# Thresholded attention and a three-way maxout feed-forward on one core: every engine's instructions put into an order written by hand

## The chip, the core and the metric

The kernel runs on one core of a Trainium2 chip. The metric is the device time of one execution in microseconds (us); lower is better. The engines are TensorE (PE in the profile, with its weight loads as PEld), VectorE (DVE), ScalarE (ACT), GpSimd (POOL) and SyncE (SP), which here only issues transfers.

## What is computed

Attention over 8 batches of 8 heads, 576 positions, head size 64, where scores more than `tau` = 0.02 below their row's maximum are dropped, and then a feed-forward layer whose hidden value is the maximum of three products:

```python
scores = scale * np.matmul(q, k.transpose(0, 1, 3, 2))
thresh = np.max(scores, axis=-1, keepdims=True) - tau
scores = np.where(scores >= thresh, scores, -1000000000.0)
scores = scores - np.max(scores, axis=-1, keepdims=True)
attn = np.exp(scores)
attn = attn / (np.sum(attn, axis=-1, keepdims=True) + 1e-09)
out = np.matmul(attn, v)                      # (8, 8, 576, 64)
x = out.transpose(0, 2, 1, 3).reshape(4608, 512)
h = np.maximum(np.maximum(x @ w1, x @ w2), x @ w3)   # 4608 x 768
y = h @ w_out                                 # 4608 x 512
```

## The kernel before

**Tiling.** The work goes by *quads*: four heads of one batch, so two quads to a batch and 16 in all. A quad is two pairs of heads (`pr` 0 and 1), and its scores are made in nine *chunks* (`idx` 0 to 8): 128 query rows of both heads of a pair, and in chunk 4 the last 64 rows of each head of both pairs. A chunk has two halves, `i` = 1 and then `i` = 0, one for each head. A half is a 128 x 576 tile of scores.

**A half's steps.** `scores` makes it in two matmuls that run side by side in the upper and the lower 64 rows of the array: one writes 256 columns and the other 320 (for `i` = 1 the upper rows write 256, for `i` = 0 they write 320). Each is recorded as two passes. Then `exponents`: VectorE takes the row maximum `nm`, and ScalarE reads the scores from PSUM into `z`. This has two forms. In the *plain* form VectorE adds `tau` to the maximum (`bm`), ScalarE applies a Prelu with a huge slope, and `numerators` is a second ScalarE pass, an exponential with a row sum. In the *masked* form ScalarE takes the exponential at once, and `numerators` is a VectorE SCALAR_TENSOR_TENSOR that drops what is under the threshold and sums. `MASKED` lists the chunks that take the masked form. Then `normalized`, once a chunk: a reciprocal on VectorE, two multiplications on GpSimd into `P` (bf16), and one DMA transpose of `P` into `ptq`, issued by SyncE.

**Other steps.** `transposed` (PSUM tile `tp`) turns q or k of a head pair by matmuls with the identity; four of them make the next quad ready. `product` (tile `o`) multiplies a head pair's `ptq` with v; two for each quad, of the quad before. `hid` (tile `ph`, 18 a batch) is one of the three hidden products for 128 of 768 columns, eight matmuls: the first of three (`wi` 0) is copied to `hm` by ScalarE, the others are folded in with a maximum by VectorE. `outp` (tile `po`, 5 a batch) makes 128 rows of the output, which ScalarE copies to `ob`.

**Order.** The loop goes over quads `g` and 18 periods `per` of a quad, one half each. In a period `other(g, per)` adds one other step: `product` for quad `g-1` at periods 3 (`O_A`) and 8 (`O_B`), `transposed` for quad `g+1` at 10, 12, 14, 16 (`T_AT`), and else the next `hid` or `outp` waiting in `todo`. A batch's 23 feed-forward steps come into `todo` after the second product of its second quad. GpSimd alone keeps the written order (`_Ordered`); on the other engines the framework's scheduler places the instructions.

**Buffers.** All PSUM tiles come from one pool of four slots that goes round (`slot`), so a tile waits until the tile four before it has been read. `z` has four buffers, `P` four, `ptq` two.

Of the kernel before, what the change touches and what calls it, by code (L numbers as in the profile page):

```python
# [11 lines left out]
F32 = mybir.dt.float32  # L12
BF16 = mybir.dt.bfloat16
AX = mybir.AxisListType.X
AF = bass_rust.ActivationFunctionType
# [4 lines left out]

STEEP = -1.0e30

MASKED = (1, 4, 7)
LAG = 0


class _Ordered:
# [20 lines left out]
def kernel(  # L48
# [18 lines left out]


    nc = tc.nc
    tensor, scalar, vector, pool = nc.tensor, nc.scalar, nc.vector, _Ordered(tc, nc.gpsimd)  # L70
    B, H, S, D = q.shape
    scale = 1.0 / math.sqrt(D)
    tau = float(tau)
# [4 lines left out]
    W = 2 * S  # L78
# [24 lines left out]
    def slot(name):  # L103
        return ps_s.tile([128, 1024], F32, name=name, tag="s")
# [52 lines left out]
    def scores(L, idx, i):  # L157

        ps = slot("sc")
        first = 256 if i == 1 else 192  # L160
        for r in range(2):
            cols = slice(first, 512) if r == 0 else slice(512, first + S)
            if i == 1:
                kc = slice(0, 256) if r == 0 else slice(0, 320)
            else:
                kc = slice(256, 576) if r == 0 else slice(320, 576)
            rows = slice(64 * r, 64 * r + 64)
            if idx != 4:
# [3 lines left out]
                tensor.matmul(ps[:, cols], t[rows, off:off + 128], L["kt", pr][rows, kc],  # L172
                              start=True, stop=True)
            else:
                for pr in range(2):
                    t = L["qt", pr] if i == r else L["qs", pr]
                    tensor.matmul(ps[64 * pr:64 * pr + 64, cols], t[rows, 256:320],  # L177
                                  L["kt", pr][rows, kc], start=True, stop=True)
        return ps[:, first:first + S]

    def exponents(L, idx, i, sc):

        masked = idx in MASKED
        n = 1 - i
        if n == 0:
            L["z"] = zz.tile([128, W], F32, name="z")
            L["sm"] = small.tile([128, 2], F32, name="sm")
        zn = L["z"][:, n * S:(n + 1) * S]
        nm = small.tile([128, 1], F32, name="nm")
        vector.tensor_reduce(out=nm, in_=sc, axis=AX, op=OP.max, negate=True)  # L190
        if masked:
            scalar.activation(out=zn, in_=sc, func=AF.Exp, bias=nm)  # L192
        else:
            bm = small.tile([128, 1], F32, name="bm")
            vector.tensor_scalar_add(bm, nm, tau)  # L195
            scalar.activation(out=zn, in_=sc, func=AF.Prelu, bias=bm, alpha=-STEEP)  # L196

    def numerators(L, idx, i, z, sm):
        masked = idx in MASKED
        n = 1 - i  # L200
        zn = z[:, n * S:(n + 1) * S]
        acc = sm[:, n:n + 1]
        if masked:
            vector.scalar_tensor_tensor(out=zn, in0=zn, scalar=thr, in1=zn,  # L204
                                        op0=OP.is_ge, op1=OP.mult, accum_out=acc)
        else:
            scalar.activation(out=zn, in_=zn, func=AF.Exp, accum_out=acc)  # L207

    def normalized(L, idx, z, sm):
        rs = small.tile([128, 2], F32, name="rs")  # L210
        vector.reciprocal(rs, sm)  # L211
# [104 lines left out]
    sc = scores(Ls[0], 0, 1)  # L316
    late = []
    for g in range(NQ):
        L = Ls[g]
        L["pt"] = pt_pool.tile([128, 9, W], BF16, name="ptq")  # L320
        for per in range(18):
            idx, i = per // 2, 1 - per % 2
            if per == 0 and g + 1 < NQ:
                Ls[g + 1] = load(*quads[g + 1])
            if per == 2 and g == 0:
                cast_v(Ls[0])
            if per == 6 and g + 1 < NQ:
                cast_v(Ls[g + 1])
            exponents(L, idx, i, sc)
            if per < 17:  # L330
                sc = scores(L, (per + 1) // 2, 1 - (per + 1) % 2)
            elif g + 1 < NQ:
                sc = scores(Ls[g + 1], 0, 1)
            late.append(lambda L=L, idx=idx, i=i, z=L["z"], sm=L["sm"]: numerators(L, idx, i, z, sm))
            if i == 0:
                late.append(lambda L=L, idx=idx, z=L["z"], sm=L["sm"]: normalized(L, idx, z, sm))
            if LAG:
                while len(late) > LAG:
                    late.pop(0)()
            other(g, per)  # L340
            if not LAG:
                while late:
                    late.pop(0)()
            if wl and (g or per >= 6) and per % 2:
                wl.pop(0)()
    while late:
        late.pop(0)()
    while todo:
        todo.pop(0)()
    o_step(NQ - 1, 0)  # L350
    o_step(NQ - 1, 1)
    while todo:
        todo.pop(0)()

# [34 lines left out]
```

## Time and profile before

| | |
|---|---|
| median of 3 runs | 574.15 us (571.12 to 575.34) |
| profiled execution | 570.12 us |
| its span, first to last instruction | 568.3 us |
| mean granted TensorE clock | 0.987 |
| busy: PE / DVE / ACT / POOL | 541.7 / 429.6 / 415.8 / 316.0 us |
| instructions | 10605 |
| 128 x 576 row maximum on VectorE | 288, 749 ns each |
| DMA transposes | 144, 3.4 us to landing |

Rows of the timeline give start, duration, engine, source line, operation, the tile written and the tile read, and in brackets how long the engine sat idle before and what ended that. Records of matmuls overlap, because the next starts before the one ahead of it has left the array; what a step costs TensorE is therefore the time from its start to the start of the next step, not the sum of its records.

### The profile page before, as it was taken

The numbers are of one execution on the slowest core, as the hardware profiler recorded it, in microseconds if no ns is written. First come the engines' busy times: TensorE is split into PE (matmuls) and PEld (weight loads), VectorE is DVE, ScalarE is ACT, GpSimd is POOL, SyncE is SP. The second block draws the span as 40 slices with busy tenths as digits, with TensorE's granted clock in tenths as the row PEclk, the third lists the DMA queues.
The fourth block names the chain that finished last, engine by engine and source line by source line (L and its number), as shares of the span: only waits on it lengthen the run. The fifth ranks groups of instructions, "written<-read, shape, count | busy, mean of one in ns | idle before, by whom it ended". The sixth has DMA issues, their size and how long they took to land.

```text
span 568.3 us, 10605 instructions
## 1 busy us (share of the span) xinstructions
PE 541.7 (95%) x3619; PEld 280.1 (49%) x3632; DVE 429.6 (76%) x976; ACT 415.8 (73%) x809; POOL 316.0 (56%) x408
## 2 busy tenths in 40 slices
PE   7786789999999999999999999999999999999997
PEld 4343445554555545554455544555455554555473
DVE  2985878886787868878788876888688786887441
ACT  2995978687877877778787778868787787777422
POOL 2798886564565646466565555646456565643300
PEclk9996989999999999999999999999999999999999
DMA  7999997758686675957868487774889446444602
GB/s 214 218 219 245 237 213 158 136 92 217 136 175 115 134 191 125 174 110 168 201 124 135 111 206 165 139 148 96 197 154 164 79 82 157 85 84 76 155 1 83
DMA packets 217109, 84.05 MB, mean 148 GB/s; under 512 B 185568, under 2 KB 212448, under 8 KB 217056
## 3 DMA queue, kind: packets, MB, share of 16 engines
q1 hardware_dynamic: 214464, 80.24, 66.9%
q0 software_dynamic: 2592, 3.15, 3.6%
q8 instruction: 28, 0.46, 0.4%
q14 instruction: 25, 0.20, 0.1%
HBM read 34.60 MB, written 9.44 MB: 77 GB/s over the span
## 4 chain that ended last, share of the span: by engine, by line
PE 79%; DVE 8%; ACT 6%; issue 3%; DMA 2%; SPq 1%; POOL 0%; POOLq 0%; ACTq 0%
PE sc L172 28%; PE ph L259 26%; PE tp L143 9%; PE o L236 8%; PE po L272 7%; DVE nm L190 4%; ACT z L207 2%; DVE z L204 2%; ACT z L196 2%; PE sc L177 2%; DMA ptq<-P 2%; ACT ob L275 1%; DMA km<-in_k_dram 1%; ACT xt L243 1%; ACT z L192 0%
## 5 line engine op out<-in xcount | busy, mean ns | idle before, releaser
L36 POOL TENSOR_SCALAR P<-z,rs 128x576 bf16<-128x576 f32 x288 | 236.1, 832 | 191.0 <-DVE rs L211 95.2
L190 DVE TENSOR_REDUCE nm<-sc 128x1 f32<-128x576 f32 x288 | 215.3, 749 | 42.4 <-PE sc L172 33.0
L172 PE MATMUL sc<-kt,qt 64*128 64x256 f32 (+1 forms) x512 | 191.6, 459 | 3.5 <-ACT z L196 3.4
L172 PE MATMUL sc<-kt,qs 64*128 64x320 f32 (+1 forms) x512 | 191.9, 459 | 3.1 <-ACT z L192 2.2
L196 ACT ACTIVATE z<-sc,bm 128x576 f32<-128x576 f32 x192 | 140.8, 736 | 68.4 <-DVE bm L195 39.7
L259 PE MATMUL ph<-xt,w 128*128 128x288 bf16 x1152 | 164.2, 287 | 0.3
L259 PEld LDWEIGHTS <-w 128*128 128x128 bf16 x1152 | 102.2, 98 | 79.0 <-issue 56.8
L207 ACT ACTIVATE z<-z 128x576 f32<-128x576 f32 x192 | 131.0, 683 | 4.2
L204 DVE SCALAR_TENSOR_TENSOR z<-z 128x576 f32<-128x576 f32 x96 | 84.1, 877 | 17.4 <-ACT z L192 16.3
L172 PEld LDWEIGHTS sc<-kt,qs 64*128 64x128 f32 x512 | 77.6, 188 | 35.9 <-ACT z L207 10.9
L192 ACT ACTIVATE z<-sc,nm 128x576 f32<-128x576 f32 x96 | 70.6, 735 | 30.8 <-DVE nm L190 29.9
L172 PEld LDWEIGHTS sc<-kt,qt 64*128 64x128 f32 x512 | 77.6, 188 | 31.2 <-issue 12.2
L36 POOL COPY qs<-qt 64x576 f32<-64x576 f32 x64 | 49.3, 770 | 28.0 <-ACT qt L147 25.3
L272 PE MATMUL po<-wo,hT 128*128 128x512 bf16 (+1 forms) x227 | 57.3, 381 | 0.7
L236 PE MATMUL o<-ptq,vb 128*64 128x288 bf16 (+2 forms) x512 | 46.2, 301 | 5.0 <-DMA ptq<-P 3.3
L266 DVE TENSOR_TENSOR hm<-ph,hm 128x576 bf16<-128x576 f32 x48 | 36.2, 755 | 15.5 <-PE ph L259 12.9
L263 ACT ACTIVATE hm<-ph 128x576 bf16<-128x576 f32 x48 | 31.0, 646 | 19.1 <-PE ph L259 19.1
L211 DVE RECIPROCAL rs<-sm 128x2 f32<-128x2 f32 x144 | 23.4, 162 | 22.1 <-ACT z L207 20.6
L266 DVE TENSOR_TENSOR hT<-ph,hm 128x576 bf16<-128x576 f32 x48 | 36.3, 757 | 3.3 <-PE ph L259 1.1
L272 PEld LDWEIGHTS <-hT 128*128 128x128 bf16 (+1 forms) x240 | 21.2, 100 | 34.9 <-issue 14.7
L236 PEld LDWEIGHTS <-vb 128*64 128x64 bf16 x512 | 25.4, 112 | 25.4 <-issue 17.2
L207 ACT ACTIVATION_READ_ACCUMULATOR z<-z 128x1 f32 x192 | 36.5, 190 | 0.0
(33 smaller groups left out, 360.6 us busy)
## 6 DMA issues: line engine op xcount, KB each, us to landing
vm<-in_v_dram SPq DMA_DIRECT2D x16, 512.0 KB, 4.7
out_dram<-ob SPq DMA_DIRECT2D x32, 256.0 KB, 2.7
qm<-in_q_dram SPq DMA_DIRECT2D x15, 512.0 KB, 4.5
km<-in_k_dram SPq DMA_DIRECT2D x15, 512.0 KB, 4.8
ptq<-P SPq DMA_TRANSPOSE x144, 3.4
w<-in_moe_w_dram POOLq DMA_DIRECT2D x12, 192.0 KB, 5.2
vr<-in_v_dram SPq DMA_DIRECT2D x32, 32.0 KB, 4.0
out_dram<-ob SPq DMA_DIRECT2D x8, 128.0 KB, 4.3
```

Source lines behind the costliest of these rows:

```text
L36: ins = fn(*a, **kw)
L143: tensor.transpose(ps[:, col:col + np_], src.rearrange("p a d -> p (a d)"), identf[:np_, :np_])
L172: tensor.matmul(ps[:, cols], t[rows, off:off + 128], L["kt", pr][rows, kc], start=True, stop=True)
L190: vector.tensor_reduce(out=nm, in_=sc, axis=AX, op=OP.max, negate=True)
L192: scalar.activation(out=zn, in_=sc, func=AF.Exp, bias=nm)
L196: scalar.activation(out=zn, in_=sc, func=AF.Prelu, bias=bm, alpha=-STEEP)
L204: vector.scalar_tensor_tensor(out=zn, in0=zn, scalar=thr, in1=zn, op0=OP.is_ge, op1=OP.mult, accum_out=acc)
L207: scalar.activation(out=zn, in_=zn, func=AF.Exp, accum_out=acc)
L236: tensor.matmul(ps[64 * i:64 * i + 64, first + a:first + e], w, x, start=(m == 0), stop=(m == 4))
L259: tensor.matmul(ps[:, a * 512:a * 512 + n], wts[wi][:, kc, f * 128:(f + 1) * 128], xt[:, kc, a * n:a * n + n], start=(kc == 0), stop=(kc = ...
L266: vector.tensor_tensor(out=dst, in0=pv, in1=hm, op=OP.max)
L272: tensor.matmul(ps[:r, :512], hT[:, f, c * 128:c * 128 + r], wo[:, f, :], start=(f == 0), stop=(f == NF - 1))
```

## The change

`_Ordered` is now laid round TensorE, ScalarE, VectorE and GpSimd, so each of the four issues exactly in the order in which the code is written, and the loop is written anew by chunks. For each chunk it issues: both maxima; the second ScalarE pass of the chunk before; the first ScalarE pass of both halves; the VectorE threshold of the chunk before; the reciprocal, multiplications and transpose of the chunk two before; two other steps; and then the scores of both halves of the next chunk. The masked form is taken by one half (`i` = 0) of six chunks rather than by both halves of three, which is six of a quad's 18 halves as before. In quads 1 to 3 the products stand at periods 9 and 15 rather than 3 and 8. `P` has six buffers.

```diff
-MASKED = (1, 4, 7)
-LAG = 0
+MASKED = (0, 1, 3, 4, 6, 7)
...
-    tensor, scalar, vector, pool = nc.tensor, nc.scalar, nc.vector, _Ordered(tc, nc.gpsimd)
+    tensor, scalar, vector, pool = (_Ordered(tc, e) for e in (nc.tensor, nc.scalar, nc.vector, nc.gpsimd))
...
-    pp = ctx.enter_context(tc.tile_pool(name="pp", bufs=4))
+    pp = ctx.enter_context(tc.tile_pool(name="pp", bufs=6))
...
+    def masked(idx, i):
+        return i == 0 and idx in MASKED
...
-    O_A, O_B, T_AT = 3, 8, (10, 12, 14, 16)
+    O_A, O_B, O_A_EARLY, O_B_EARLY, T_AT = 3, 8, 9, 15, (10, 12, 14, 16)
...
-        if g > 0 and per == O_A:
+        if g > 0 and per == (O_A if g > 3 else O_A_EARLY):
             o_step(g - 1, 0)
-        elif g > 0 and per == O_B:
+        elif g > 0 and per == (O_B if g > 3 else O_B_EARLY):
             o_step(g - 1, 1)
...
+            cur = [(L, idx, i, z, sm) for i in (1, 0)]
+            bias = [maximum(idx, i, sc[1 - i]) for i in (1, 0)]
+            for c in prev:
+                if not masked(c[1], c[2]):
+                    numerators(*c)
+            for i in (1, 0):
+                exponents(idx, i, z, sc[1 - i], bias[1 - i])
+            for c in prev:
+                if masked(c[1], c[2]):
+                    numerators(*c)
+            if late:
+                normalized(*late)
+            late = (prev[0][0], prev[0][1], prev[0][3], prev[0][4]) if prev else None
+            prev = cur
+            other(g, 2 * idx)
+            other(g, 2 * idx + 1)
+            nxt = (L, idx + 1) if idx < 8 else (Ls[g + 1], 0) if g + 1 < NQ else None
+            if nxt:
+                sc = [scores(*nxt, 1), scores(*nxt, 0)]
+            if wl and (g or idx >= 3):
                 wl.pop(0)()
```

`maximum` holds what was the VectorE part of `exponents`. Below, the order in which the built program has the instructions (an instruction of the changed kernel carries the line of the helper, L35).

TensorE before, in the second half of a quad in the middle of the program; `sc` is one half's scores, `tp` a transposition, `ph` a hidden product, and the number behind a name tells tiles apart:

```order
L259 MATMUL ph_3298<-xt_2145,w2_65 128x288
L172 MATMUL sc_3320<-kt_2923,qt_2877 128x320
L172 MATMUL sc_3320<-kt_2923,qs_2879 128x256
L143 MATMUL tp_3323<-identf_58,qm_2952 128x128 x2
L143 MATMUL tp_3323<-identf_58,qr_2953 128x64
L143 MATMUL tp_3323<-identf_58,qm_2952 128x128 x2
L172 MATMUL sc_3338<-kt_2923,qs_2879 128x256
L172 MATMUL sc_3338<-kt_2923,qt_2877 128x320
L259 LDWEIGHTS w0_63
```

TensorE now, at the same stage of a quad:

```order
L35 MATMUL ph_3311<-xt_2104,w1_64 128x288
L35 MATMUL sc_3321<-kt_2901,qs_2856 128x256
L35 MATMUL sc_3321<-kt_2901,qt_2854 128x320
L35 MATMUL sc_3324<-kt_2901,qs_2856 128x320
L35 MATMUL sc_3324<-kt_2901,qt_2854 128x256
L35 MATMUL tp_3347<-identf_58,km_2922 128x128 x2
L35 MATMUL tp_3347<-identf_58,kr_2923 128x64
L35 MATMUL tp_3347<-identf_58,km_2922 128x128 x2
L35 LDWEIGHTS w2_65
```

Before, one half's scores stood between every two other steps; now a chunk's two halves follow each other, and then two other steps, here a transposition and a hidden product.

VectorE before, near a quad's first product (`xt<-o` is the copy of the product, `nm` the maximum, `bm` the maximum plus `tau`, `rs` the reciprocal):

```order
L204 SCALAR_TENSOR_TENSOR z,sm<-z 128x576
L190 TENSOR_REDUCE nm<-sc 128x1
L204 SCALAR_TENSOR_TENSOR z,sm<-z 128x576
L211 RECIPROCAL rs<-sm 128x2
L190 TENSOR_REDUCE nm<-sc 128x1
L195 TENSOR_SCALAR bm<-nm 128x1
L240 CAST xt<-o 128x576
L190 TENSOR_REDUCE nm<-sc 128x1
```

VectorE now, at such a product:

```order
L35 TENSOR_REDUCE nm<-sc 128x1
L35 TENSOR_SCALAR bm<-nm 128x1
L35 TENSOR_REDUCE nm<-sc 128x1
L35 SCALAR_TENSOR_TENSOR z,sm<-z 128x576
L35 RECIPROCAL rs<-sm 128x2
L35 TENSOR_TENSOR hT<-ph,hm 128x576
L35 CAST xt<-o 128x576
L35 TENSOR_REDUCE nm<-sc 128x1
```

Both maxima of a chunk now stand ahead of everything else of the chunk, and the threshold pass behind them belongs to the chunk before.

ScalarE before, in a stretch of hidden products (`z<-sc` is the first pass, `z,sm<-z` the second):

```order
L196 ACTIVATE z<-sc,bm 128x576
L207 ACTIVATE z,sm<-z 128x576
L196 ACTIVATE z<-sc,bm 128x576
L207 ACTIVATE z,sm<-z 128x576
L192 ACTIVATE z<-sc,nm 128x576
L263 ACTIVATE hm<-ph 128x576
L192 ACTIVATE z<-sc,nm 128x576
```

ScalarE now:

```order
L35 ACTIVATE z,sm<-z 128x576 x2
L35 ACTIVATE z<-sc,bm 128x576
L35 ACTIVATE z<-sc,nm 128x576
L35 ACTIVATE hm<-ph 128x576
L35 ACTIVATE z,sm<-z 128x576
L35 ACTIVATE z<-sc,bm 128x576
L35 ACTIVATE z<-sc,nm 128x576
```

A second pass used to follow its own first pass; it now waits for the next chunk and stands ahead of that chunk's two first passes.

More of the change, by code (lines that the diff above doesn't have):

```diff
@@ L179, in scores, with maximum, exponents @@
         return ps[:, first:first + S]
[L181 to L188, printed above, removed]
+    def masked(idx, i):
+        return i == 0 and idx in MASKED
+    def maximum(idx, i, sc):
         nm = small.tile([128, 1], F32, name="nm")
         vector.tensor_reduce(out=nm, in_=sc, axis=AX, op=OP.max, negate=True)
-        if masked:
-            scalar.activation(out=zn, in_=sc, func=AF.Exp, bias=nm)
-        else:
-            bm = small.tile([128, 1], F32, name="bm")
-            vector.tensor_scalar_add(bm, nm, tau)
-            scalar.activation(out=zn, in_=sc, func=AF.Prelu, bias=bm, alpha=-STEEP)
+        if masked(idx, i):
+            return nm
+        bm = small.tile([128, 1], F32, name="bm")
+        vector.tensor_scalar_add(bm, nm, tau)
+        return bm
+    def exponents(idx, i, z, sc, bias):
+        zn = z[:, (1 - i) * S:(2 - i) * S]
+        if masked(idx, i):
+            scalar.activation(out=zn, in_=sc, func=AF.Exp, bias=bias)
+        else:
+            scalar.activation(out=zn, in_=sc, func=AF.Prelu, bias=bias, alpha=-STEEP)
     def numerators(L, idx, i, z, sm):
-        masked = idx in MASKED
         n = 1 - i
@@ L202, in numerators @@
         acc = sm[:, n:n + 1]
-        if masked:
+        if masked(idx, i):
             vector.scalar_tensor_tensor(out=zn, in0=zn, scalar=thr, in1=zn,
@@ L315 @@
         transposed(Ls[0], *a)
-    sc = scores(Ls[0], 0, 1)
-    late = []
+    sc = [scores(Ls[0], 0, 1), scores(Ls[0], 0, 0)]
+    late, prev = None, []
     for g in range(NQ):
@@ L320 @@
         L["pt"] = pt_pool.tile([128, 9, W], BF16, name="ptq")
-        for per in range(18):
-            idx, i = per // 2, 1 - per % 2
-            if per == 0 and g + 1 < NQ:
+        for idx in range(9):
+            if idx == 0 and g + 1 < NQ:
                 Ls[g + 1] = load(*quads[g + 1])
-            if per == 2 and g == 0:
+            if idx == 1 and g == 0:
                 cast_v(Ls[0])
-            if per == 6 and g + 1 < NQ:
+            if idx == 3 and g + 1 < NQ:
                 cast_v(Ls[g + 1])
[L329 to L344, printed above, removed]
@@ L345 @@
+            if late:
[8 more added lines that the diff above has]
+            if wl and (g or idx >= 3):
                 wl.pop(0)()
-    while late:
-        late.pop(0)()
+    normalized(*late)
@@ L348 @@
+    for c in prev:
+        numerators(*c)
+    normalized(prev[0][0], prev[0][1], prev[0][3], prev[0][4])
     while todo:
         todo.pop(0)()
-    o_step(NQ - 1, 0)
-    o_step(NQ - 1, 1)
+    for pr in range(2):
+        o_step(NQ - 1, pr)
     while todo:
```

2 lines of the change are left out of this document (added).

## The prediction

> **What bounds the kernel now.** I read the page's busy times first, then busy time by stretches of the program, then the chain that ended last, then TensorE's timeline inside one period. The page's slices:
>
> ```profile
> PE   7786789999999999999999999999999999999997
> PEclk9996989999999999999999999999999999999999
> ```
>
> TensorE leaves gaps only in the first six or seven slices of 14.2 us and at the end. Busy time by stretches (the columns are length, then busy time of each engine with its instructions, granted clock, share of the DMA engines, GB/s) and four rows of the chain that mark where quads and batches start:
>
> ```profile
> core 0: us, PE busy (x) PEld busy (x) DVE busy (x) ACT busy (x) POOL busy (x), PEclk, DMA share, GB/s
> 12.23:34.94 22.71, 17.54 (x102) 8.00 (x100) 20.30 (x53) 19.88 (x41) 16.37 (x21) 1.00 1.02 223
> 34.94:65.33 30.39, 22.99 (x142) 11.78 (x142) 22.00 (x56) 22.32 (x45) 27.11 (x39) 0.83 1.21 232
> 65.33:94.06 28.73, 25.16 (x169) 12.79 (x170) 23.44 (x58) 23.70 (x47) 23.14 (x32) 0.94 0.97 195
> 94.06:127.43 33.37, 33.37 (x237) 17.68 (x237) 28.01 (x66) 25.27 (x50) 18.76 (x24) 1.00 0.69 133
> 285.09:352.27 67.18, 67.02 (x453) 33.99 (x456) 53.99 (x122) 51.96 (x102) 38.25 (x48) 1.00 0.73 150
> ```
>
> ```profile
> 200.35 1.40 PE po L272 x6
> 202.49 1.70 PE o L236 x20
> ...
> 285.09 1.09 PE ph L259 x8
> ...
> 352.27 1.09 PE ph L259 x8
> ```
>
> The first three windows are quads 0, 1 and 2, the fourth quad 3, the fifth a whole batch of two quads. From quad 3 on TensorE is busy for all of the time (33.37 of 33.37, 67.02 of 67.18), VectorE for 80% and ScalarE for 77%. So thirteen quads (3 to 15) last as long as TensorE's list of steps, and only what shortens that list, or makes TensorE wait, moves the time. What each step costs, from start to start:
>
> ```profile
> 284.28 0.48 PE L172 MATMUL sc<-kt,qs 64*128 64x256 f32 x1
> ...
> 285.02 1.15 PE L259 MATMUL ph<-xt,w 128*128 128x288 bf16 x8
> 286.10 0.53 PE L172 MATMUL sc<-kt,qs 64*128 64x320 f32 x1
> ...
> 286.84 0.44 PE L143 MATMUL tp<-identf,km 128*128 128x128 f32 x2
> ...
> 287.78 0.48 PE L172 MATMUL sc<-kt,qt 64*128 64x256 f32 x1
> ```
>
> One half's scores take 0.74 us, a hidden product 1.08, a transposition 0.94; by the chain an output step takes 1.40 and a product 1.70. A batch is 36 x 0.74 + 18 x 1.08 + 8 x 0.94 + 5 x 1.40 + 4 x 1.70 = 67.4 us, against 67.18 measured: the list is complete.
>
> **The change, part by part.** *Scores of both halves back to back.* Alone, a half takes 0.74 us although its longer matmul pair covers the array for less; the trace before has a few places where the scheduler let halves follow each other:
>
> ```profile
> 40.40 0.53 PE L172 MATMUL sc<-kt,qt 64*128 64x320 f32 x1
> ...
> 42.10 0.43 PE L177 MATMUL sc<-kt,qs 64*64 64x256 f32 x2
> ```
>
> ```profile
> 51.75 0.79 PE L172 MATMUL sc<-kt,qt 64*128 64x256 f32 x1
> ...
> 53.97 0.69 PE L143 MATMUL tp<-identf,qm 128*128 128x128 f32 x2
> ```
>
> Three halves in a row took 1.70 us, so each further one (1.70 - 0.74) / 2 = 0.48 and a pair 1.22. The second place is one pair at half the clock, 2.22 us, or 1.11 at the full one. I take 1.17. [...] A chunk saves 1.48 - 1.17 = 0.31 us, 18 chunks 5.6 us. Bounds: 1.11 saves 6.7 us, 1.22 saves 4.7.
>
> *Two other steps back to back.* The last feed-forward of the trace before runs hidden products without anything between:
>
> ```profile
> 539.76 17.84 PE L259 MATMUL ph<-xt,w 128*128 128x288 bf16 x144
> 557.44 6.75 PE L272 MATMUL po<-wo,hT 128*128 128x512 bf16 x29
> ```
>
> 144 matmuls in 17.68 us are 0.98 us for eight, 0.10 less than between scores. Not every second step is such a one (products and transpositions come between), so I take 0.06 x 17 chunks = 1.0 us a batch, between 0 and 1.7. TensorE's list falls by 6.6 us to 60.6 us a batch, 3.37 us a chunk.
>
> *The chain from scores to scores.* With two other steps in every chunk the four PSUM slots go round once a chunk, so a half's scores must wait until the same half of the chunk before has been read. That is the new wait, and all of the next chunk's work on TensorE queues behind it. Its links, by rows:
>
> ```profile
> 283.46 0.74 ACT L196 ACTIVATE z<-sc,bm 128x576 f32<-128x576 f32 x1 [1.61 <-PE sc L172]
> 283.46 0.76 DVE L190 TENSOR_REDUCE nm<-sc 128x1 f32<-128x576 f32 x1
> ...
> 284.26 0.15 DVE L195 TENSOR_SCALAR bm<-nm 128x1 f32<-128x1 f32 x1
> 284.28 0.18 PEld L172 LDWEIGHTS sc<-kt,qs 64*128 64x128 f32 x1 [0.17 <-ACT z L196]
> ...
> 285.13 0.76 DVE L190 TENSOR_REDUCE nm<-sc 128x1 f32<-128x576 f32 x1 [0.72 <-PE sc L172]
> ```
>
> ```profile
> 530.24 0.15 DVE L195 TENSOR_SCALAR bm<-nm 128x1 f32<-128x1 f32 x1
> ...
> 530.49 0.74 ACT L196 ACTIVATE z<-sc,bm 128x576 f32<-128x576 f32 x1 [0.78 <-DVE bm L195]
> ```
>
> From the start of a half's scores to its maximum 0.85 us (284.28 to 285.13); maximum to the addition of `tau` 0.80; addition to first pass 0.25; first pass to the weight load that waits for it 0.82 (283.46 to 284.28). The second half of an unmasked chunk, whose maximum starts some 0.88 us after the first one's (0.80, and a part of the addition), is ready for overwriting at 0.85 + 0.88 + 0.80 + 0.25 + 0.82 = 3.60 us, and its turn in the next pair comes about 0.5 us after that pair begins: the pair may begin at 3.1 us. In a masked chunk the addition falls away and the pair may begin at about 2.9. TensorE needs at least 1.17 + 0.94 + 1.08 = 3.2 us before it gets there. So the chain hides, but with only 0.1 us to spare in a quad's three unmasked chunks and 0.3 in the masked. VectorE's 54.0 and ScalarE's 52.0 us a batch would be 87% and 84% of 62 us, in fixed order, so sometimes an operation comes late. I allow 1.4 us of waits a batch (0 if all is hidden; one second pass in the way in each unmasked chunk, at the 683 ns below, would be 6 x 0.68 = 4.1): 62.0 us, 2.6 us less for each quad. Thirteen quads: **-34 us**.
>
> ```profile
> L36 POOL TENSOR_SCALAR P<-z,rs 128x576 bf16<-128x576 f32 x288 | 236.1, 832 | 191.0 <-DVE rs L211 95.2
> ...
> L207 ACT ACTIVATE z<-z 128x576 f32<-128x576 f32 x192 | 131.0, 683 | 4.2
> ...
> ptq<-P SPq DMA_TRANSPOSE x144, 3.4
> ```
>
> *Masked halves.* 6 of 18 halves as before, so 96 threshold passes and 192 second passes stay: 0. They are spread more evenly, which takes no work away.
>
> *Second pass, reciprocal, `P` and transpose later.* GpSimd's two multiplications and SyncE's issue move a chunk or two back, behind the chunk's first half on VectorE. Six buffers of `P` and four of `z` cover two chunks. Chunk 8's reciprocal comes in chunk 1 of the next quad, two chunks (6.8 us) before the second product in chunk 4; two multiplications of 0.83 us and 3.4 us to landing leave 1.7 us to spare: 0. If it lands late, TensorE stops at the product, as here:
>
> ```profile
> 50.41 1.06 PE L236 MATMUL o<-ptq,vb 128*64 128x256 bf16 x8 [2.06 <-DMA ptq<-P]
> ```
>
> *Products later in quads 1 to 3.* This removes that stop and the half clock near it. Quad 1 then goes by GpSimd, which was busy for 27.1 us of 30.4 (weight loads stand in its queue): -3. Quad 0 has VectorE at 20.3 of 22.7: 0. In quad 2 the first feed-forward starts nine periods later, so four of its steps leave the quad (28.7 to 26 us: -3) and fill later periods that stood empty, 4 x 1.08 = +4. Together **-2 us**.
>
> *End.* From the last scores to the product that needs their transpose it took 10.0 us:
>
> ```profile
> 529.00 0.53 PE L172 MATMUL sc<-kt,qs 64*128 64x320 f32 x1
> ...
> 538.98 0.63 PE L236 MATMUL o<-ptq,vb 128*64 128x256 bf16 x8 [1.27 <-DMA ptq<-P]
> ```
>
> That stays about the same, but TensorE will have only two output steps and one product, 4.5 us, to put there. I put the longer gap and slower matmuls behind it at **+2 us** (0 to 4).
>
> Sum: 570.1 - 34 - 2 + 2 = 536 us for the profiled execution. The median of the runs shown lay 4.0 us over it; with half of that I forecast **538 us**.
>
> **Rivals.** *The chain shows.* If VectorE or ScalarE is late by 0.2 us more in each chunk, a quad gains 0.8 us rather than 2.6: 538 + 13 x 1.8 = 561 us. For it: the 0.1 us to spare. Against it: both engines are idle for a tenth of the time and may work ahead by most of a chunk.
>
> *Slower: a convoy on ScalarE.* The second passes of the chunk before stand ahead of the first passes. If they start only when the maximum is there, the chain grows by 1.33 of them on average, 0.9 us: 2.9 + 0.9 = 3.8 and more in a chunk, and with 0.1 us for the other waits 3.9, against 67.18 / 18 = 3.73 now: 13 x 9 x 0.17 = +20, so 592 us. It decides once the chain exceeds 3.73 us, that is 0.6 us of lateness in every chunk. For it: fixed order and no slack in PSUM. Against it: the second passes need nothing from this chunk, and ScalarE has about 0.6 us of idle time a chunk to do them before.
>
> *The clock falls in the first quads.* The granted clock was halved in quad 1 when TensorE had idled for 2.4 us:
>
> ```profile
> 45.23 0.80 PE L177 MATMUL sc<-kt,qt 64*64 64x320 f32 x2 [2.36 <-ACT z L196]
> ```
>
> ```profile
> 45.00:50.00 5.00, 3.01 (x18) 1.32 (x19) 1.78 (x6) 4.17 (x10) 4.91 (x8) 0.50 1.24 231
> 50.00:55.00 5.00, 4.59 (x22) 2.80 (x22) 2.74 (x9) 1.23 (x2) 3.71 (x6) 0.51 1.37 227
> ```
>
> Now a chunk of quads 0 to 2 has one gap of about 1.3 us instead of two short ones. If that suffices, a pair takes 2.22 us and each of the 27 chunks may lose up to 0.5 us: +13, 551 us. Against it: quad 0 ran at 1.00 with TensorE busy for 77%. [...]
>
> *The pair saves nothing* because the matmuls of the second half wait for their slot one by one: only the 1.0 us a batch is left, 13 x 0.5 = 7 us, 563 us.
>
> **How the numbers follow.** Forecast (538) 0.62, chain shows (561) 0.14, clock (551) 0.08, no pair (563) 0.05, slower (592) 0.11. The low end takes all bounds at their best: 67.4 - 6.7 - 1.7 = 59.0 us a batch and no waits, 13 x 4.1 = 53 rather than 34 us: 519 us. The high end, 562, takes in the chain rival. A measurement of this kernel can tell about 1% (6 us) from no change. Values from 568 to 580 count as no change, where the chain is twice as late as in its rival: 0.04 of its 0.14. Slower is the convoy and worse: 0.11. Faster: 0.85.
>
> **What the profile will show.** Right: a pair of halves 1.1 to 1.25 us from start to start; a batch of 60.6 to 63 us with TensorE still busy for over 97%; VectorE and ScalarE near 85%; no stop at a product in quads 1 to 3. Wrong: TensorE idle before scores, released by the first pass, for more than 0.2 us in most chunks (chain or convoy); a clock under 0.9 in quads 0 to 2; a product that waits for `ptq`.

## The result, and the profile after

The median fell from 574.75 us (571.12 to 583.30, four runs of the kernel before on the same chip) to **546.14 us** (541.97 to 547.87, four runs): a ratio of 0.951, 95% interval 0.943 to 0.959. The forecast was 538, the range 519 to 562. Runs more than 1.5% above the fastest of their kernel (583.30 here, 545.10 in the first experiment) count as slow and are left out of the ratios. The profiled execution took 547.87 us, 546.1 of them the span.

The slices of 13.7 us in the page of the changed kernel, TensorE and its granted clock:

```profile
PE   7778689999999999999999999999999999998697
PEclk9988689999999999999999999999999999999799
```

The gaps at the start are still there, the clock is low in slices 3 to 6, and at the end TensorE has a gap and a low clock that the kernel before did not have. The busy time by stretches (columns as before): quads 0 to 2, then a whole batch of two quads, all cut where a quad's first maximum starts:

```profile
11.20:33.06 21.86, 18.27 (x108) 9.75 (x105) 20.97 (x51) 20.39 (x43) 15.17 (x22) 1.00 1.11 237
33.06:66.16 33.10, 23.61 (x136) 13.41 (x136) 23.01 (x57) 22.33 (x47) 26.93 (x39) 0.78 1.28 201
66.16:91.23 25.07, 22.33 (x152) 13.06 (x149) 22.38 (x56) 21.16 (x45) 19.71 (x28) 0.89 1.12 225
313.24:377.28 64.04, 62.76 (x467) 38.45 (x466) 52.40 (x125) 51.19 (x105) 34.85 (x50) 1.00 0.73 158
```

The same view for quads 3 to 14 as one stretch, and for the rest of the program, first of before and then of after:

```profile
94.06:497.18 403.12, 402.22 (x2714) 204.03 (x2725) 323.97 (x734) 311.83 (x607) 229.04 (x288) 1.00 0.70 144
497.18:568.30 71.12, 65.59 (x470) 38.16 (x471) 38.31 (x80) 35.52 (x67) 16.98 (x22) 0.99 0.35 80
```

```profile
91.23:473.08 381.85, 373.36 (x2765) 228.46 (x2762) 311.98 (x737) 303.13 (x612) 205.75 (x290) 1.00 0.74 153
473.08:546.10 73.02, 63.08 (x457) 39.35 (x455) 36.64 (x79) 33.64 (x64) 16.50 (x23) 0.95 0.36 82
```

So the 22.2 us that the span lost are made up of: the start -1.0, quad 0 -0.8 (22.7 to 21.9), quad 1 **+2.7** (30.4 to 33.1), quad 2 -3.7 (28.7 to 25.1), quads 3 to 14 **-21.3** (403.1 to 381.9), and quad 15 with the end +1.9 (71.1 to 73.0). A batch lasts 63.6 us on average (381.85 / 6), where 62.0 was predicted, and in quad 1 stands a long stop at a product, which the prediction had ruled out for quads 1 to 3.

**The list of steps.** TensorE's timeline in the middle of the program, where nothing waits:

```profile
235.82 0.48 PE L35 MATMUL sc<-kt,qt 64*128 64x256 f32 x1
...
236.99 0.44 PE L35 MATMUL tp<-identf,qm 128*128 128x128 f32 x2
...
237.84 1.14 PE L35 MATMUL ph<-xt,w 128*128 128x288 bf16 x8
238.91 0.48 PE L35 MATMUL sc<-kt,qs 64*128 64x256 f32 x1
```

The pair of halves takes 1.17 us from start to start (235.82 to 236.99), a transposition with a hidden product behind it 0.85 (to 237.84, 0.94 before) and that hidden product 1.07. With two hidden products at 2.06, two output steps at 2.69 and a product at 1.70 (read in the same way elsewhere), a batch is 18 x 1.17 + 3 x 2.06 + 12 x 1.07 + 6.9 + 4 x 1.70 + 8 x 0.85 = **60.6 us**. That is the list that was predicted. Of the other 3.0 us of a batch's 63.6, 0.7 are no wait. The four hidden products that left quad 2 now stand in quads 3 to 14, which have 112 of them instead of 108 by the order of the loop. The view of the tile `ph` shows it, first of before and then of after: VectorE and ScalarE read 72 + 36 = 108 of them before and 75 + 38 = 113 after, one of these at a cut between two stretches.

```profile
94.06:497.18 403.12, 125.56 (x865) 54.45 (x72) 23.23 (x36) 1.00 0.70 144
91.23:473.08 381.85, 125.52 (x901) 55.88 (x75) 24.13 (x38) 1.00 0.74 153
```

So the list of these twelve quads is 6 x 60.6 + 4 x 1.07 = 367.9 us, and their waits are 381.85 - 367.9 = 14.0 us, 2.3 a batch. About two thirds of them lie at two kinds of places; the rest are smaller waits ahead of scores, which were not followed up.

**Quad's end.** VectorE and TensorE where chunk 8 gives way to chunk 0 of the next quad; it looks the same where quads 5, 6, 7, 11, 13 and 15 begin:

```profile
247.71 1.19 DVE L35 SCALAR_TENSOR_TENSOR z<-z 128x576 f32<-128x576 f32 x1
...
248.90 0.73 DVE L35 COPY kt<-tp 128x576 f32<-128x576 f32 x1
249.56 0.74 DVE L35 TENSOR_TENSOR hT<-ph,hm 128x576 bf16<-128x576 f32 x1
250.22 0.74 DVE L35 TENSOR_REDUCE nm<-sc 128x1 f32<-128x576 f32 x1
```

```profile
248.23 0.48 PE L35 MATMUL sc<-kt,qt 64*128 64x256 f32 x1
...
249.69 2.12 PE L35 MATMUL ph<-xt,w 128*128 128x288 bf16 x16 [0.21 <-DVE kt L35]
252.06 0.48 PE L35 MATMUL sc<-kt,qs 64*128 64x256 f32 x1 [0.26 <-ACT z L35]
...
253.43 1.15 PE L35 MATMUL ph<-xt,w 128*128 128x288 bf16 x8
```

The first maximum of chunk 0 starts at 250.22, 1.99 us after its scores began (248.23) instead of 0.85: a threshold pass, the copy of `kt` and the maximum of a hidden product with `hm` stand ahead of it. The pair before took 1.46 us, the two hidden products 2.37 and the next pair 1.37, against 1.17, 2.06 and 1.17: 0.8 us at each such place. Only 0.47 of them show as idle; the rest stands in the trace as busy time.

**Two neighbours that depend on each other.** TensorE's timeline at a quad's second product, and then, in the same quad, at the first output step:

```profile
393.54 0.54 PE L35 MATMUL ph<-xt,w 128*128 128x288 bf16 x3
394.68 0.77 PE L35 MATMUL ph<-xt,w 128*128 128x288 bf16 x5 [0.60 <-ACT xt L35]
395.38 0.48 PE L35 MATMUL sc<-kt,qt 64*128 64x256 f32 x1
```

```profile
377.72 1.24 PE L35 MATMUL po<-wo,hT 128*128 128x512 bf16 x5
379.66 0.39 PE L35 MATMUL po<-wo,hT 128*128 128x512 bf16 x1 [0.69 <-DVE hT L35]
379.98 0.48 PE L35 MATMUL sc<-kt,qs 64*128 64x256 f32 x1
```

A hidden product stands right behind the product whose copy `xt` it reads, and an output step right behind the last hidden product, whose `hT` it reads. Before, one half's scores stood between them. The first costs 0.77 us (393.54 to 395.38 is 1.84 instead of 1.07), the second 0.86 (377.72 to 379.98 is 2.26 instead of 1.40). Each occurs three times in quads 3 to 14, the first in quads 10, 12 and 14 and the second in quads 6, 12 and 14, 4.9 us in all: until the four late steps are worked off, the second product of a batch is followed by a step of the batch before.

### The profile page after: what moved, and what is told of

The parts are those of the page before. It is cut to its first block, busy times and chain, and to the rows that moved or that the text cites. A ratio compares the mean times of both kernels' runs of the same rounds, so it can differ in the third digit from the quotient of the medians.

```text
span 546.1 us, 10703 instructions
## 1 busy us (share of the span) xinstructions
PE 508.3 (93%) x3632; PEld 308.5 (56%) x3632; DVE 416.5 (76%) x976; ACT 403.2 (74%) x809; POOL 288.2 (53%) x408
## 4 chain that ended last, share of the span: by engine, by line
PE 66%; DVE 20%; ACT 6%; DMA 3%; issue 2%; POOL 2%; SPq 0%; POOLq 0%; ACTq 0%; DVEq 0%
PE sc L35 23%; PE ph L35 19%; DVE nm L35 10%; PE po L35 8%; PE o L35 8%; PE tp L35 8%; ACT z L35 5%; DVE z L35 4%; DMA ptq<-P 3%; DVE hm L35 2%; DVE bm L35 1%; DVE kt L35 1%; DVE hT L35 1%; POOL P L35 1%; ACT hm L35 1%
## 5 line engine op out<-in xcount | busy, mean ns | idle before, releaser
L35 POOL TENSOR_SCALAR P<-z,rs 128x576 bf16<-128x576 f32 x288 | 215.5, 761 | 210.7 <-ACT z L35 170.0
L35 DVE TENSOR_REDUCE nm<-sc 128x1 f32<-128x576 f32 x288 | 216.0, 750 | 55.4 <-PE sc L35 55.1
L35 ACT ACTIVATE z<-sc,bm 128x576 f32<-128x576 f32 x192 | 142.0, 741 | 91.0 <-DVE bm L35 68.2
L35 PE MATMUL sc<-kt,qs 64*128 64x256 f32 (+2 forms) x640 | 188.8, 439 | 6.5 <-ACT z L35 6.3
L35 PE MATMUL sc<-kt,qt 64*128 64x320 f32 (+2 forms) x640 | 188.3, 451 | 5.0 <-ACT z L35 2.9
L35 PE MATMUL ph<-xt,w 128*128 128x288 bf16 x1152 | 159.6, 288 | 3.9 <-DVE kt L35 1.9
L35 PEld LDWEIGHTS <-w 128*128 128x128 bf16 x1152 | 109.5, 98 | 46.0 <-issue 20.2
L35 ACT ACTIVATE z<-z 128x576 f32<-128x576 f32 x192 | 130.5, 683 | 0.0
L35 PEld LDWEIGHTS sc<-kt,qs 64*128 64x128 f32 (+1 forms) x640 | 94.2, 182 | 37.7 <-ACT z L35 22.1
L35 PEld LDWEIGHTS sc<-kt,qt 64*128 64x128 f32 (+1 forms) x640 | 93.5, 182 | 30.3 <-ACT z L35 13.3
L35 DVE SCALAR_TENSOR_TENSOR z<-z 128x576 f32<-128x576 f32 x96 | 80.6, 840 | 0.6 <-ACT z L35 0.6
L35 ACT ACTIVATE z<-sc,nm 128x576 f32<-128x576 f32 x96 | 70.9, 738 | 0.0
L35 PE MATMUL po<-wo,hT 128*128 128x512 bf16 (+1 forms) x240 | 57.2, 381 | 3.4 <-DVE hT L35 3.4
L35 PE MATMUL o<-ptq,vb 128*64 128x288 bf16 (+2 forms) x512 | 46.5, 302 | 10.8 <-DMA ptq<-P 9.4
L35 DVE TENSOR_TENSOR hm<-ph,hm 128x576 bf16<-128x576 f32 x48 | 35.8, 746 | 18.1 <-PE ph L35 10.8
L35 POOL COPY qs<-qt 64x576 f32<-64x576 f32 x64 | 42.8, 669 | 9.8 <-ACT qt L35 6.3
L35 ACT ACTIVATE hm<-ph 128x576 bf16<-128x576 f32 x48 | 31.2, 651 | 16.3 <-PE ph L35 15.9
L35 PEld LDWEIGHTS <-hT 128*128 128x128 bf16 (+1 forms) x240 | 22.2, 100 | 33.2 <-issue 6.3
L35 PEld LDWEIGHTS <-vb 128*64 128x64 bf16 x512 | 25.0, 112 | 27.6 <-issue 13.3
L35 ACT ACTIVATION_READ_ACCUMULATOR z<-z 128x1 f32 x192 | 38.6, 201 | 0.0
L35 DVE TENSOR_TENSOR hT<-ph,hm 128x576 bf16<-128x576 f32 x48 | 36.0, 749 | 2.4 <-PE ph L35 1.4
L35 DVE TENSOR_SCALAR bm<-nm 128x1 f32<-128x1 f32 x192 | 29.5, 154 | 6.6
```

What stands on the lines that cost most here:

```text
L35: ins = fn(*a, **kw)
```

## The experiments

Each kernel changes the one after, unless the text says otherwise; ratios are to the kernel before, run beside it on the same chip.

**VectorE's order at the quad's end.** In `transposed`, the copy of `kt` for the pair of heads that ends in chunk 8 goes to ScalarE:

```diff
-            vector.tensor_copy(out=t, in_=ps[:, 192:768])
+            if pr == 1:
+                scalar.activation(out=t, in_=ps[:, 192:768], func=AF.Copy)
+            else:
+                vector.tensor_copy(out=t, in_=ps[:, 192:768])
```

> The changed kernel, but the k transposition of a quad's second head pair (the one in chunk 8) is copied out by ScalarE rather than VectorE. Theory (at a quad's end VectorE is the late engine: chunk 8 holds the threshold pass of chunk 7, an addition for both halves, this copy and a maximum of the feed-forward, about 4.1 us against TensorE's 3.1): with 0.67 us taken off, the waits of TensorE between chunk 8 and chunk 1 of the next quad fall from 0.8 us a quad to under 0.3, about 8 us over the program, 538 us. Rival (ScalarE's first passes are late there by themselves): ScalarE has 0.65 us more to do in the same chunk, the waits grow to over 1.2 us a quad and the time by 5 us or more, 551 us.

537.54 us (535.29 to 545.10), ratio 0.935 (0.928 to 0.941), and the profiled span 536.3. TensorE's idle time ahead of scores at the quads' ends is at most 0.17 us at a time, while the wait behind the second product is what it was (0.61 us). Quads 3 to 14 by stretches:

```profile
86.92:463.69 376.77, 371.47 (x2751) 227.07 (x2759) 304.84 (x724) 308.74 (x622) 204.79 (x289) 1.00 0.77 157
```

They are 5.1 us shorter than after (381.85). The medians lie about 9 us apart; of the other 4.7 us between the two profiled spans, 2.6 lie in quad 1, whose length changes between executions anyway (see below), and the rest in quads 0, 2 and 15. So moving one copy of 0.73 us, off an engine that is busy for 80% of the time, was worth 5 us in the middle of the program, since it stood ahead of a maximum.

**The dependent neighbours.** From quad 4 on the second product goes one period later, behind a chunk's last step, and no output step is taken right behind the last hidden product in the same chunk:

```diff
-    O_A, O_B, O_A_EARLY, O_B_EARLY, T_AT = 3, 8, 9, 15, (10, 12, 14, 16)
+    O_A, O_B, O_A_EARLY, O_B_EARLY, T_AT = 3, 9, 9, 15, (10, 12, 14, 16)
...
-        elif todo:
+        elif todo and not (len(todo) == 5 and last[0] == (g, per - 1) and per % 2):
             todo.pop(0)()
+            last[0] = (g, per)
```

> The changed kernel, but two pairs of neighbours that depend on each other are taken apart: the second product of a quad stands at period 9 rather than 8 from quad 4 on, so that the first hidden product, which reads its copy, comes a chunk later; and the first output step never stands in the same chunk right behind the last hidden product. Theory (TensorE waits 0.6 to 0.8 us at each of the two places, once a batch): both waits vanish, 1.4 us a batch, 9 to 10 us in all, 537 us. Rival (VectorE paces the chunks, and these waits only show its lateness): the waits turn up elsewhere and the time stays within 3 us of 546.

535.63 us (534.13 to 536.00), ratio 0.933 (0.929 to 0.938). By stretches, quads 3 to 14, and the rest of the program:

```profile
88.75:463.78 375.03, 369.45 (x2729) 226.67 (x2738) 311.37 (x734) 300.88 (x611) 205.85 (x291) 1.00 0.78 158
463.78:533.80 70.02, 64.12 (x479) 40.63 (x479) 37.87 (x81) 34.26 (x65) 16.46 (x23) 1.00 0.38 85
```

The waits at the dependent neighbours are gone, and nearly all idle time that is left in quads 3 to 14 lies at the quads' ends. But the edit does more than the theory says. Its second part leaves a period empty in five batches, so three feed-forward steps that stood in quads 6 to 10 move behind the last quad: five output steps wait there instead of two. Of the 6.8 us that quads 3 to 14 lose (381.85 to 375.03), about 3 are these three steps, so the neighbours account for some 4 us. The rest of the program is 3.0 us shorter (73.02 to 70.02) although it holds three steps more: they fill the gap in which TensorE waited for the last transposes, and the stop there is gone. The two parts were not run apart, so the 10 us must not be put down to the neighbours alone. (Another 2.4 us between the profiled spans lie in quads 1 and 2, which the edit does not touch.)

**The pair by itself.** The two halves are put apart again, with the other two steps between and behind them; everything else stays in the written order:

```diff
             other(g, 2 * idx)
+            sc = [scores(*nxt, 1)]
             other(g, 2 * idx + 1)
-                sc = [scores(*nxt, 1), scores(*nxt, 0)]
+                sc.append(scores(*nxt, 0))
```

> The changed kernel, but the scores of a chunk's two halves are issued apart again, each behind one other step. Theory (the gain is TensorE's shorter list): each half costs 0.74 us and each other step its lone cost, so a batch goes back by 18 x 0.31 + 1 = 6.6 us, to about 67 us with waits that hide in the longer list, and the program to 568 to 575 us. Rival (the gain comes from the order on VectorE and ScalarE): it stays under 555 us.

584.31 us (583.65 to 588.19), ratio 1.020 (1.014 to 1.026): slower than before, though not clearly by 2%, and slower than either theory had it. By stretches, a batch:

```profile
338.10:408.56 70.46, 69.28 (x465) 35.22 (x466) 52.07 (x124) 51.58 (x106) 35.89 (x50) 1.00 0.68 146
```

A half takes 0.74 us again and the transposition 0.94, so the list is that of before: 67.2 us, and 1.1 for the one more hidden product that this batch holds. Waits of 2.2 us come on top, about as many as in the kernel after. The gain sits in the pairs; the written order without them loses 11 us.

**Products in the first quads.** They go back to periods 3 and 8:

```diff
-    O_A, O_B, O_A_EARLY, O_B_EARLY, T_AT = 3, 8, 9, 15, (10, 12, 14, 16)
+    O_A, O_B, O_A_EARLY, O_B_EARLY, T_AT = 3, 8, 3, 8, (10, 12, 14, 16)
```

> The changed kernel, but the products of quads 1 to 3 stand at periods 3 and 8 as in all other quads. Theory (in quad 1 the transposes of quad 0 land 17 us late, because the transfers of the first 70 us are more than the queues carry, so a product that needs them stops TensorE wherever it stands): the stop comes earlier and is longer, 10 us or more, quad 1 is no shorter than 33 us, but the feed-forward begins half a quad sooner; 546 to 554 us. Rival (the later products caused the stop): quad 1 falls below 30 us and the time below 543.

553.92 us (551.49 to 555.51), ratio 0.965 (0.960 to 0.971). Quad 1 by stretches:

```profile
32.63:67.24 34.61, 24.61 (x142) 14.33 (x140) 22.48 (x57) 22.28 (x47) 25.40 (x37) 0.75 1.15 213
```

Quad 1 took 34.6 us, and quad 2, which gets its four steps back, 30.0. The later products are worth about 8 us in this order, where the prediction had put them at 2.

**Quad 1's stop.** In the profile after, quad 1's second product waited for its transposed `P`. TensorE's timeline there, SyncE's, and the line on landing times in the view of the tile `ptq`:

```profile
59.59 1.06 PE L35 MATMUL o<-ptq,vb 128*64 128x256 bf16 x8 [5.33 <-DMA ptq<-P]
```

```profile
43.92 13.79 SPq L218 DMA_TRANSPOSE ptq<-P  x3
```

```profile
DMA to landing us min/median/max: 3.2/3.4/13.3
```

Three transposes held SyncE's queue for 13.79 us, and the longest time from issue to landing is 13.3 us, four times the median. Beside them the loads of the feed-forward's weights are under way: four of them were issued by GpSimd between 43.94 and 55.32 us. The experiment takes these loads out of the middle of quad 1: nine in quad 0, three at the start of quad 1, six in quad 3.

```diff
-            if wl and (g or idx >= 3):
+            if wl and (g == 0 or (g == 1 and idx < 3) or g > 2):
```

> The changed kernel, but the 18 weight loads are spread otherwise: 9 in quad 0, 3 in quad 1, 6 in quad 3, rather than 6, 9 and 3 in quads 0, 1 and 2. Theory (in quad 1 the loads of weights, of the next quad and the transposes are more than the DMA engines carry, so transposes take 9 to 13 us to land instead of 3.4 and the second product stops TensorE): flights in quad 1 fall to under 7 us, the stop of 5 to 6 us shrinks to under 2, quad 1 from 33 to under 28 us, 540 us. Rival (the transposes are late because SyncE issues them in order behind loads whose buffers are not free yet): flights and the stop stay, 544 to 548 us.

544.93 us (542.11 to 546.35), ratio 0.948 (0.944 to 0.952). TensorE at the same product, and the landing times:

```profile
56.99 0.63 PE L35 MATMUL o<-ptq,vb 128*64 128x256 bf16 x8 [1.27 <-DMA ptq<-P]
```

```profile
DMA to landing us min/median/max: 3.2/3.6/12.8
```

The stop fell from 5.33 to 1.27 us and quad 1 from 33.1 to 26.9 us. The longest time to landing did not fall below 7 us, as the theory had it, but stayed at 12.8, and the medians of the two kernels could not be told apart. Either the gain is given back elsewhere, or the stop isn't always as long. So both kernels ran once more on one chip, the kernel after unchanged:

> The changed kernel as it is, timed beside the next one on the same chip, since the medians of the two (546.1 and 544.9 us) lay closer than their profiled spans (546.1 and 540.3 us). Both theories of the next run: 542 to 548 us.

> The kernel with the weight loads spread otherwise (9, 3 and 6 in quads 0, 1 and 3), again. Theory (the shorter stop in quad 1, 33.1 to 26.9 us in the profiles, less 1.8 us that quad 0 grew, is a gain in every execution): 4 to 6 us under the changed kernel of the same call. Rival (the stop in quad 1 differs from execution to execution, and the profile of the changed kernel caught a long one): under 2 us apart.

The kernel after: 545.61 us (540.38 to 547.67, six runs), ratio 0.951 (0.947 to 0.955). With the moved loads: **541.02** (540.59 to 541.52, four runs), ratio 0.943 (0.940 to 0.945). Quad 1 by stretches in the unchanged kernel's second profile:

```profile
33.10:58.67 25.57, 21.91 (x142) 11.63 (x140) 22.57 (x56) 21.89 (x47) 24.82 (x35) 0.87 1.23 232
```

The same kernel had quad 1 at 33.10 us in one profile and 25.57 in the other, and its other quads agree; the two spans (546.1 and 538.6) differ by as much as quad 1. So this stop comes and goes from execution to execution. That it also makes the spread of 7 us in the runs without a profile is likely, but not shown. With the moved loads quad 1 took 26.9, 26.7 and, in the kernel with all three repairs below, 26.4 us, with stops of 1.3 to 1.4 us; in the eight profiles here that have the loads as they were and the products at periods 9 and 15, it took 25.6 to 33.1, with stops of 0 to 5.3. In these profiles, which differ in other edits too, the moved loads take away the long stops rather than the short ones. Their runs spread over 0.9 us on this chip, but over 4.2 on the other.

**Is it the order, or the pairs alone?** Three engines get their order from the scheduler again, and the program text with its pairs stays:

```diff
-    tensor, scalar, vector, pool = (_Ordered(tc, e) for e in (nc.tensor, nc.scalar, nc.vector, nc.gpsimd))
+    tensor, scalar, vector, pool = nc.tensor, nc.scalar, nc.vector, _Ordered(tc, nc.gpsimd)
```

> The changed kernel, but only GpSimd keeps the written order; on TensorE, VectorE and ScalarE the framework's scheduler places the instructions again. Theory (what counts is that TensorE gets scores in pairs; the order by hand is what keeps them so): the scheduler pulls other steps between the halves, and the time goes up with the number of halves that stand alone, to 560 us or more if half of them do. Rival (the order written in the loop is enough, the fixed issue adds nothing): pairs stay, and the time is within 4 us of 546.

599.33 us (597.94 to 602.57), ratio 1.042 (1.039 to 1.046): the slowest kernel here. My reason for it fell: the scheduler did not pull the halves apart. By stretches a batch, and the waits in it:

```profile
345.34:418.18 72.84, 65.39 (x465) 36.88 (x462) 52.71 (x123) 51.53 (x104) 34.96 (x48) 1.00 0.66 139
```

```profile
ACT z L199 <- DVE bm L190: 13.3, 11, 2.6
DVE z L206 <- ACT z L197: 11.9, 11, 1.7
```

(The columns are the sum in us, how often, and the longest.) VectorE's threshold pass waits for ScalarE's first pass ahead of the next maximum; ScalarE then waits for that maximum, and TensorE's weight loads for ScalarE (9.1 us in 12 places). This is a convoy like that of the prediction's slower rival, but with VectorE's threshold passes at its head rather than ScalarE's second passes. Leaving TensorE alone to the scheduler tells whose order it was:

> The changed kernel, but TensorE alone is left to the framework's scheduler, while ScalarE, VectorE and GpSimd keep the written order. Theory (what cost 53 us when the scheduler had all three was the order on VectorE and ScalarE, where a threshold pass that waits for ScalarE stood ahead of the next maxima; pairs stayed on TensorE): within 6 us of 546. Rival (the order on TensorE was what cost): 570 us or more.

545.18 us (543.28 to 548.34), ratio 0.950 (0.946 to 0.954): nothing lost. So it is the order on VectorE and ScalarE that the 53 us hang on; which of the two it takes was not run apart.

**Which halves are masked.** The chunks 1, 4 and 7 get both halves masked, as before the change:

```diff
-MASKED = (0, 1, 3, 4, 6, 7)
+MASKED = (1, 4, 7)
...
-        return i == 0 and idx in MASKED
+        return idx in MASKED
```

> The changed kernel, but the masked form is again taken by both halves of chunks 1, 4 and 7. Theory of the prediction (the masked halves are as many, so where they stand costs nothing): 544 to 549 us. Rival (chunks 2, 5 and 8 then have two threshold passes of the chunk before in VectorE's queue, 0.75 us more in chunk 8, which is the late one, while chunks 1, 4 and 7 have none): TensorE's waits at a quad's end double, 555 us or more.

557.99 us (556.50 to 561.64), ratio 0.973 (0.969 to 0.977): 12 us slower than after, with the same work, as the rival had it. By stretches, quads 3 to 14:

```profile
86.61:483.55 396.94, 379.64 (x2749) 226.17 (x2758) 307.16 (x736) 304.15 (x610) 204.93 (x290) 1.00 0.72 148
```

VectorE and ScalarE have as much to do as in the other kernels, but in lumps: behind a second product TensorE idles 1.06 us for the `xt` copy instead of 0.60. With the same list of 367.9 us, the waits of quads 3 to 14 come to 29.0 us instead of 14.0; how they are spread was not followed up.

**All three repairs together** (`kt` copy, neighbours apart, moved loads):

> The changed kernel with three edits together: the copy moved to ScalarE in chunk 8, the two pairs of dependent neighbours taken apart, and the weight loads spread otherwise. Theory (the three kinds of wait are separate): the gains add, about 9 + 10 us and what the weight loads bring (5 us if that theory holds): 522 to 528 us, a batch of 60.5 to 61.5 us with TensorE idle for under 0.5 us. Rival (they share one cause, the lateness of VectorE): the gains overlap, 532 us or more.

**525.46 us** (524.17 to 526.61), ratio 0.915 (0.911 to 0.918), the fastest kernel of this case. By stretches, a batch:

```profile
298.93:360.31 61.38, 61.11 (x456) 37.40 (x455) 50.37 (x121) 51.07 (x104) 34.03 (x49) 1.00 0.88 168
```

This batch lies 0.8 us over the list of 60.6, the next one (61.16) 0.6. Alone the three were worth about 9, 10 and 4 us, together 20 against the kernel after (545.61): they nearly add up. What the second one gains at the end of the program is in this sum too.

## Why the prediction was right, and where its sizes were off

- **Where the profiled time missed.** The terms came to 536 us, and the profiled execution took 547.87. Of these nearly 12 us, 5.9 lie in quads 3 to 14 (12 x -2.6 + 4 = -27.2 forecast, -21.3 measured), 5.7 in quad 1 (-3 and +2.7), and some 3 at the end; the start and quads 0, 2 and 15 gave back the rest.
- **TensorE's list sets the time: right.** The pair at 1.17 us, the list at 60.6, and a kernel that comes down to it (61.2) once its waits are removed. Putting the halves apart gave the old list back. The 1.0 us for steps that are no longer alone came out as well, though most of it in the transpositions (8 x 0.09) rather than in the hidden products.
- **"I allow 1.4 us of waits a batch": too little, 2.3.** Over six batches this is 5.6 us, about half of what the profiled time missed. The chain from scores to scores was sized rightly: between chunks inside a quad it shows in few places. What it left out is that a fixed order puts things *ahead* of the maximum (the `kt` copy at the quad's end; moving it gave 5.1 us in six batches), and that two steps of one feed-forward can become neighbours (0.77 and 0.86 us, in three places each). Both could be read from the order of the built program, had I looked at chunk 8 and at a second product with the question of what each instruction needs from the one ahead. The first two repairs gave about 9 and 10 us by the medians, 5.1 and some 4 of them at these places.
- **"TensorE still busy for over 97%": right, and a poor sign.** 62.76 of 64.04 us is 98%, while 2.4 us of that batch were waits (its list is 60.6 and one hidden product more, 61.7). Start-to-start times showed them.
- **Masked halves, "0": wrong.** Spread evenly they are worth 12 us under this order. The sum of work was right; I took even spreading for neutral, though the chain had 0.1 us to spare. It is luck that the change spread them: with the halves in lumps the same sum would have stood for a kernel that took 558.
- **Quad 1, "-3": no fixed number.** +2.7 in one profile, -4.8 in another. The condition was in the prediction ("If it lands late, TensorE stops at the product"), but I reckoned with 3.4 us to landing from the median. The kernel before had a longest time to landing of 7.0 us to warn me. Quad 2's -3 came out at -3.7, quad 0's 0 at -0.8. In quad 2 the second product stands seven periods later, not nine as I wrote; that four steps leave the quad is right.
- **End, "+2 us (0 to 4)": too little, about 5.** Quad 15 and the end together took 1.9 us longer, although quad 15 itself gained some 3 us by its shorter list. "That stays about the same" is the step that failed: from the last scores to the product that needs their transpose it took 13.3 us (501.37 to 514.62) instead of 10.0. The stop ahead of that product grew from 1.27 to 3.81 us, and the clock fell to half within it, for 6.8 us (0.50 from 512.20 to 519.03):

```profile
501.37 0.48 PE L35 MATMUL sc<-kt,qs 64*128 64x256 f32 x1
...
514.62 1.06 PE L35 MATMUL o<-ptq,vb 128*64 128x256 bf16 x8 [3.81 <-DMA ptq<-P]
...
515.97 19.45 PE L35 MATMUL ph<-xt,w 128*128 128x288 bf16 x144
535.25 6.76 PE L35 MATMUL po<-wo,hT 128*128 128x512 bf16 x30
```

The 144 matmuls took 19.3 us (515.97 to 535.25) instead of 17.7. Where more output steps are left for this gap, as in the second repair, the stop is gone.

- **The rivals.** The chain shows: mainly at quads' ends, 0.8 us at each of seven, and for another reason than lateness in every chunk. The pair saves nothing: rejected by its 1.17 us, and by the split, which lost 38 us against the kernel after. The convoy: not in this kernel. I had put the fixed order down as speaking for it; the runs show the reverse, since it is the kernel with the scheduler's order that has it. The clock: it was under 0.9 in quads 1 and 2 (0.78 and 0.89), as that rival said; but in the second profile quad 1 took 25.6 us at 0.87, less than the 27 that I expected at full clock, so 13 us is far too much.
- **The signs.** The pair (1.17 us) and TensorE's share (98%) came as the prediction said, and TensorE's idle time before scores stayed under 0.2 us in most chunks. A batch of 63.6 us lies just above the 63 that it named, VectorE and ScalarE were at 82% and 80% rather than near 85%, and two of its three signs of being wrong did show: the clock under 0.9 in quads 1 and 2, and a product that waits for `ptq`.

## What to carry to other kernels

When the bound is one engine's list, look for steps that take less next to each other than apart (here the two halves of a chunk, 1.17 us against 1.48), and check what stands next to what. In an order written by hand put first what others wait for, and leave at least one step between two that depend on each other: here the change came to -28 us with such an order, to +25 with a scheduler's on three engines, and to -49 where the waits left in it were taken out too. A busy share of 98% was no proof here that nothing waited (about 2.4 us of a batch of 64.0 were waits); add up the list from undisturbed steps and compare it with the length. Loads that were only needed later, taken away from transposes that something waited for, gave 4.6 us by the medians of one chip (545.61 to 541.02).

## What the runs showed of the hardware

The transposes' time to landing was not a constant in the kernel after: 3.4 us in the median, 13.3 at the longest, counted from the issue; three of them held SyncE's queue for 13.79 us. Busy time by stretches, in a window of 5 us ahead of that stop (the last two columns are the DMA engines' share and GB/s):

```profile
45.00:50.00 5.00, 4.97 (x36) 2.68 (x30) 4.34 (x10) 3.84 (x8) 4.96 (x8) 1.00 1.37 141
```

The share was higher there than in quad 0, and less was moved: 141 GB/s at 1.37, against 237 GB/s at 1.11. What made the transposes late was not measured by itself; that the transfers were more than the queues or the DMA engines carry, as two of the theories have it, no run showed. With the weight loads moved away the long stops did not occur in three profiles and the median fell by 4.6 us on one chip, but the longest times to landing were still 12.8, 10.5 and 12.0 us, and one profile with the loads as they were had a longest of only 8.6.

In the kernel after, the granted clock fell to half after 1.5 us without a matmul. Two neighbouring windows, and TensorE's last row ahead of the fall with the first one behind it:

```profile
34.40:37.81 3.41, 1.43 (x8) 0.60 (x8) 3.36 (x9) 1.86 (x5) 3.29 (x5) 0.99 1.23 218
37.81:44.64 6.83, 5.94 (x36) 3.48 (x38) 6.36 (x16) 6.82 (x15) 6.69 (x11) 0.50 1.22 238
```

```profile
35.91 0.43 PE L35 MATMUL sc<-kt,qt 64*128 64x320 f32 x1
38.49 0.79 PE L35 MATMUL sc<-kt,qs 64*128 64x256 f32 x1 [2.15 <-ACT z L35]
```

The last record ahead of the fall ends at 36.34 us (35.91 + 0.43), the clock was 0.50 from 37.81 on, and it stayed there for 6.83 us. In the first window it was 0.99, with TensorE busy for 1.43 us. What made it fall was not shown.
